# One of three maxout products folded into the output: differences of weights, W1 Wout added to y, and a new hand order

## The chip, the cores and the metric

The kernel runs on one core of one Trainium2 chip. The metric is the device time of one execution in microseconds; the median of three runs is given with the lowest and the highest. The core has five engines that run side by side and wait for each other by semaphores: TensorE (PE in the profile; PEld is its weight load), VectorE (DVE), ScalarE (ACT), GpSimd (POOL) and SyncE (SP), which here only issues DMAs. TensorE writes to PSUM, eight banks of 128 x 512 float32; the other tiles lie in SBUF.

## What is computed

Attention with a sliding window of 128 and 4 sink keys, over batch 4, 8 heads, 768 positions and head size 64, and then a feed-forward layer whose hidden value is the largest of three products (3072 tokens, model width 512, hidden width 768). Inputs and output are float32; the kernel works in bfloat16 with float32 accumulation.

```
scores = scale * np.matmul(q, k.transpose(0, 1, 3, 2))
keep = is_sink | in_window
scores = np.where(keep, scores, -1000000000.0)
scores = scores - np.max(scores, axis=-1, keepdims=True)
a = np.exp(scores)
a = a / (np.sum(a, axis=-1, keepdims=True) + 1e-09)
attn_out = np.matmul(a, v)
x = np.ascontiguousarray(attn_out.transpose(0, 2, 1, 3)).reshape(B * S, H * D)
h = np.maximum(np.maximum(x @ w1, x @ w2), x @ w3)
return (h @ w_out).astype(np.float32)
```

## The kernel before, in words

The 3072 tokens are cut into 12 chunks of 256 queries, three to a batch entry. A chunk passes through these steps, each a small function that records its instructions:

- `load(ci, what)`: three DMAs of float32 k, q and v, 512 KB each, from SP's queue. Two buffers of each. Some carry a `gate`: a tiny GpSimd write into the buffer that the DMA must wait for.
- `cast_qk`, `cast_k`, `cast_v`: to bfloat16, on whatever engine the call names. `turn` and `turn2` transpose q and k on TensorE (chunks 0 to 3), `turn_dma` by a transposing DMA (from chunk 4).
- `score`, `expo`, `mask`: key-by-query scores into two PSUM banks for each pair of heads, exponentials by ScalarE, the window mask as a product on VectorE. From chunk 6 (`NEW`) `score4`, `expo4` and `mask4` do this with smaller key blocks. `sink_score` and `sink_v` add the four sink keys.
- `av_open`, `av`, `norm`: the weighted sum of v (with a column of ones for the row sum) and the division on VectorE, which gives `x_sb`. `xpose` (TensorE) or `xpose_dma` transposes x into `xT`.
- `ffn_h(ci, fp, wi)`: one PSUM bank of x W for weight wi and the pair fp of 128-column blocks, eight matmuls of 128x256. For wi = 0 ScalarE copies it into `h_sb`; for wi = 1 and 2 VectorE takes the maximum with what is there. With `then=False` the copy or maximum is recorded later by `ffn_max`.
- `ffn_y`, or `y_open`, `y_turn` and `y_out`: h times Wout, six depth steps of 128x512 for each of two halves of the chunk. `y_turn` does it in tiles of 64 rows, in two turns. `store` writes the chunk out.

PSUM banks are handed out by `bank` and returned by `give`, in the order of recording, first in, first out: which earlier tile a new one must wait for is fixed by the order in which the steps are written. Each engine works through its own instructions in that same order. Nothing is scheduled automatically: up to chunk 4 the order is a list of calls written by hand, and from there on a loop over i (lines 897 to 956), whose iteration holds the attention of chunk n = i + 1, the h of chunk i, the y of chunk m = i - 1, the casts of chunk i + 2 (all on GpSimd except q, which ScalarE casts) and the loads of chunk i + 3. "The iteration of chunk n" below is that one.

The three weights W1, W2, W3 are loaded by GpSimd's queue in nine parts (`load_w(wi, c0, c1)`), Wout in two (`load_wo`). While they and the first chunks arrive, TensorE starts with matmuls of zeros (`warm`) and masks added ahead of the scores (`premask`).

Inside a chunk the queries lie with even and odd ones apart, since a DMA row holds two neighbouring positions. The matmul of `ffn_h` reads `xT` through a rearranged view (lines 518 to 526), so that the output rows pair up again for the store.

Of the kernel before, what the change touches and what calls it, by code (L numbers as in the profile page):

```python
# [16 lines left out]
def kernel(  # L17
# [13 lines left out]
    nc = tc.nc  # L31
# [17 lines left out]
    with tc.manual_schedule():  # L49
# [71 lines left out]
        def cast_v(ci, n, i, eng):  # L121
# [5 lines left out]
            for h in range(2):  # L127
                x, y = 64 * h + 32 * i, 64 * n + 32 * h
                eng.tensor_copy(  # L129
                    vb[ci % RING][x:x + 32, n, :, 0:D], raws[ci, "v"][y:y + 32, :, i])  # L130
# [109 lines left out]
        def masks2():  # L240
            nc.gpsimd.memset(keep, 1.0)
            for h in range(2):
                for i in range(2):
# [3 lines left out]
                        base=64 * h + i, pattern=[[-64, 2], [-1, 2], [-2, 32]],  # L247
# [3 lines left out]
                        base=-64 * h - i, pattern=[[64, 2], [1, 2], [2, 32]],  # L251
# [45 lines left out]
        def load_wo():  # L297
            x = moe_w_out.rearrange("(a p) f -> p a f", p=128)
            for a in range(0, FB, FB // 2):
                nc.gpsimd.dma_start(out=wo[:, a:a + FB // 2], in_=x[:, a:a + FB // 2])  # L300

# [68 lines left out]
        def expo4(ci, p):  # L370
            e, st = es[ci, p]
            for a in range(2):
                dst = e[:, a] if ci % CPB else e[:, a, 1:].rearrange("q s (j r) -> q (s j) r", j=2)
                nc.scalar.activation(dst, st[a], AF.Exp, scale=scale)  # L374
# [33 lines left out]
        def sink_score(ci):  # L408
# [18 lines left out]
            nc.scalar.activation(e, st, AF.Exp, scale=scale)  # L427
# [83 lines left out]
        def ffn_h(ci, fp, wi, cuts=1, eng=nc.scalar, then=True):  # L511
# [3 lines left out]
            for f in range(2):  # L515
                c0 = (2 * fp + f) * 128
                for ds in range(DS):
                    x = xTs[ci][:, ds]
                    if ci < NEW:
                        x = x.rearrange("q t (i r) -> q i t r", i=2)  # L520
                    else:
                        x = (x.rearrange("q t c -> q (t c)")
                             .rearrange("q (j i r) -> q i j r", i=2, r=32))
                    nc.tensor.matmul(  # L524
                        hp[:, f].rearrange("q (i t r) -> q i t r", i=2, r=x.shape[3]),
                        lhsT=w_sb[wi][:, ds, c0:c0 + 128], rhs=x,
# [17 lines left out]

        def ffn_y(ci, t, eng=None):
# [6 lines left out]
            for fb in range(FB):  # L552
                nc.tensor.matmul(yp, lhsT=hs[ci][:, fb, t * 128:(t + 1) * 128], rhs=wo[:, fb],  # L553
                                 start=(fb == 0), stop=(fb == FB - 1))
# [9 lines left out]
        def y_turn(ci, turn, cols):  # L564
# [6 lines left out]
            for fb in range(FB):  # L571
                for c in range(0, 128, cols):
                    for a in range(2):
                        t = a ^ turn
                        hp = slice(64 * a, 64 * a + 64)
                        x = t * 128 + c
                        nc.tensor.matmul(  # L577
                            yps[ci][t][c:c + cols], lhsT=hs[ci][hp, fb, x:x + cols],
                            rhs=wo[hp, fb], start=(turn == 0 and fb == 0),
                            stop=(turn == 1 and fb == FB - 1), skip_group_check=True)  # L580
# [13 lines left out]
        def ffn_y_part(ci, t, c0, c1, eng):  # L594
# [3 lines left out]
            for fb in range(FB):  # L598
                nc.tensor.matmul(yp, lhsT=hs[ci][:, fb, t * 128:(t + 1) * 128],  # L599
                                 rhs=wo[:, fb, c0:c1], start=(fb == 0), stop=(fb == FB - 1))  # L600
# [3 lines left out]
        def store(ci):  # L604
            nc.sync.dma_start(
                out=out[ci * 256:ci * 256 + 256].rearrange("(p i) d -> p i d", i=2), in_=ys[ci])

        def store_half(ci, i, c0=0, c1=d_model, eng=None):
            dst = out[ci * 256:ci * 256 + 256].rearrange("(p i) d -> p i d", i=2)
# [10 lines left out]

        def cast(ci):
            if ci >= NCH:
                return
            assert ci >= NEW
            if ci == NEW:
                for g in range(2):
                    cast_qk(ci, "q", g, nc.gpsimd)
            for n in range(2):
                for h in range(2):
                    for i in range(2):  # L630
                        cast_k(ci, n, h, i, nc.gpsimd)
            if ci > NEW and ci % CPB == 1:
                sink_k(ci // CPB)
            for n in range(2):
                for i in range(2):
# [364 lines left out]
```

## Time and profile before

| | us |
|---|---|
| median of 3 runs (lowest to highest) | 175.3 (175.07 to 176.21) |
| span of the profiled execution, first to last instruction | 173.5 |
| median less that span | 1.8 |

The page names no other time for the profiled execution than its span; the 1.8 us stand for what lies around it. TensorE is busy nearly all the time, and its granted clock is full in all slices. The table's first row of a group gives busy time, mean length of one instruction, then the engine's idle time ahead of such instructions and what ended it. A mean length of a matmul (0.27 us for the h matmuls) is longer than its share of TensorE's time, since matmuls overlap; the chain of work, in order of time, gives the true pace.

```profile
L524 PE MATMUL h_ps<-xT,w 128*128 128x256 bf16 x864 | 101.2, 273 | 0.1
...
L536 ACT CAST h_sb<-h_ps 128x512 bf16<-128x512 f32 x35 | 20.5, 585 | 52.2 <-PE h_ps L524 52.2
```

### The profile page before, as it was taken

Reading aid. Unit: us, or ns where it says so; the run is one execution under the profiler, and the core shown is the slowest. Engines: PE = TensorE matmul, PEld = TensorE weight load, DVE = VectorE, ACT = ScalarE, POOL = GpSimd, SP = SyncE. Lnnn points to the kernel's source line nnn. Section 1 sums busy time; section 2 is a strip of 40 time slices with the busy share of each in tenths; the row PEclk is TensorE's granted clock in tenths of the full one; section 3 lists DMA queues with packets and bytes.
Section 4 is the critical chain, followed back from the end, with each engine's and each line's share of the span. In section 5 each row is a group of like instructions: output and inputs, shape, how many; then the busy total and the mean of one; then the engine's idle time right before and its main releaser. Section 6 shows DMA issues by size and latency. Waiting matters only on the chain.

```text
span 173.5 us, 5418 instructions
## 1 busy us (share of the span) xinstructions
PE 167.7 (97%) x2225; PEld 129.2 (74%) x2225; DVE 125.1 (72%) x262; ACT 88.8 (51%) x183; POOL 110.1 (63%) x193
## 2 busy tenths in 40 slices
PE   7979999999999999999999999999999999999992
PEld 2546889857695697797797797797897896896871
DVE  3187856696697985986877977877778876776361
ACT  4598554587944615817726717627636516510210
POOL 7389507445399999999999999999998700000000
PEclk9999999999999999999999999999999999999999
DMA  4999999999996999988999969969999119017303
GB/s 134 300 289 198 216 217 252 219 274 290 292 210 118 250 264 180 252 188 220 264 186 247 264 165 254 257 163 238 257 176 274 32 34 376 21 35 272 121 2 121
DMA packets 71545, 35.22 MB, mean 203 GB/s; under 512 B 27488, under 2 KB 69984, under 8 KB 71520
## 3 DMA queue, kind: packets, MB, share of 16 engines
q1 hardware_dynamic: 65824, 31.60, 79.0%
q0 software_dynamic: 5552, 3.15, 12.8%
q8 instruction: 17, 0.28, 0.7%
q10 hardware_dynamic: 144, 0.13, 0.2%
q14 instruction: 8, 0.07, 0.1%
HBM read 25.17 MB, written 6.29 MB: 181 GB/s over the span
## 4 chain that ended last, share of the span: by engine, by line
PE 93%; DVE 3%; ACT 1%; issue 0%
PE h_ps L524 55%; PE y_ps L577 11%; PE y_ps L553 7%; PE o L471 7%; PE st L357 3%; PE warm L203 3%; PE st L331 3%; PE pt L138 2%; ACT e_sb L398 1%; PE o L453 1%; DVE x_sb L484 1%; PE sk L423 1%; PE y_ps L599 1%; DVE vb L123 1%; PE xt L496 1%; PE st L311 0%
## 5 line engine op out<-in xcount | busy, mean ns | idle before, releaser
L524 PE MATMUL h_ps<-xT,w 128*128 128x256 bf16 x864 | 101.2, 273 | 0.1
L524 PEld LDWEIGHTS <-w 128*128 128x128 bf16 x864 | 81.9, 98 | 9.9 <-issue 0.3
L540 DVE TENSOR_TENSOR h_sb<-h_sb,h_ps 128x512 bf16<-128x512 bf16 (+1 forms) x74 | 49.3, 671 | 20.0 <-PE h_ps L524 16.0
L536 ACT CAST h_sb<-h_ps 128x512 bf16<-128x512 f32 x35 | 20.5, 585 | 52.2 <-PE h_ps L524 52.2
L129 POOL CAST vb<-v_raw 32x512 bf16<-32x512 f32 x48 | 36.7, 764 | 2.8 <-DMA v_raw<-in_v_dram 0.6
L90 POOL CAST k_bf<-k_raw 32x512 bf16<-32x512 f32 x48 | 29.5, 614 | 2.2
L398 ACT ACTIVATE e_sb<-st 128x512 bf16<-128x512 f32 (+1 forms) x48 | 23.1, 588 | 0.7 <-PE st L331 0.7
L484 DVE TENSOR_TENSOR x_sb<-o,rc 128x256 bf16<-128x256 f32 x48 | 20.4, 424 | 1.6
L577 PE MATMUL y_ps<-wo,h_sb 64*64 64x512 bf16 (+1 forms) x312 | 21.1, 377 | 0.0
L471 PE MATMUL o<-vb,e_sb 128*128 128x65 bf16 x352 | 16.8, 193 | 0.4 <-ACT e_sb L398 0.4
L471 PEld LDWEIGHTS <-e_sb 128*128 128x128 bf16 x352 | 14.6, 97 | 2.8 <-issue 0.8
L123 POOL CAST vb<-v_raw 64x512 bf16<-64x512 f32 x18 | 12.4, 691 | 5.8 <-DMA v_raw<-in_v_dram 5.2
L389 DVE TENSOR_TENSOR e_sb<-e_part,msk 128x1024 bf16<-128x1024 bf16 x16 | 13.5, 865 | 3.1 <-ACT e_part L374 3.0
L406 DVE TENSOR_TENSOR e_sb<-e_sb,msk 128x1024 bf16<-128x1024 bf16 (+1 forms) x18 | 13.3, 756 | 2.1 <-ACT e_sb L398 2.0
L577 PEld LDWEIGHTS <-h_sb 64*64 64x64 bf16 (+1 forms) x312 | 9.9, 106 | 5.0
L374 ACT ACTIVATE e_part<-st 128x384 bf16<-128x384 f32 x32 | 13.1, 496 | 0.5 <-PE st L357 0.5
L553 PE MATMUL y_ps<-wo,h_sb 128*128 128x512 bf16 x54 | 13.0, 380 | 0.0
L481 DVE RECIPROCAL rc<-o 128x4 f32<-128x4 f32 x48 | 8.3, 174 | 3.5 <-PE o L471 3.4
L118 POOL CAST k_bf<-k_raw 128x512 bf16<-128x512 f32 x6 | 3.8, 647 | 9.6 <-DMA k_raw<-in_k_dram 9.4
L553 PEld LDWEIGHTS <-h_sb 128*128 128x128 bf16 x54 | 4.8, 97 | 5.6 <-DVE h_sb L540 0.9
L118 ACT CAST q_bf<-q_raw 128x512 bf16<-128x512 f32 x13 | 7.6, 621 | 2.0 <-DMA q_raw<-in_q_dram 1.9
L427 ACT ACTIVATE e_sink<-sk 128x256 bf16<-128x256 f32 x8 | 3.1, 389 | 10.0 <-PE sk L423 10.0
(90 smaller groups left out, 144.2 us busy)
## 6 DMA issues: line engine op xcount, KB each, us to landing
k_raw<-in_k_dram SPq DMA_DIRECT2D x11, 512.0 KB, 5.7
v_raw<-in_v_dram SPq DMA_DIRECT2D x11, 512.0 KB, 5.8
q_raw<-in_q_dram SPq DMA_DIRECT2D x10, 512.0 KB, 6.5
out_dram<-y_sb SPq DMA_DIRECT2D x9, 512.0 KB, 3.1
w<-in_moe_w_dram POOLq DMA_DIRECT2D x9, 256.0 KB, 6.6
q_raw<-in_q_dram SPq DMA_DIRECT2D x4, 256.0 KB, 7.7
out_dram<-y_sb SPq DMA_DIRECT2D x1, 1024.0 KB, 5.2
wo<-in_moe_w_out_dram POOLq DMA_DIRECT2D x2, 384.0 KB, 7.4
```

The source lines that it names most:

```text
L90: f(bfs[ci, "k"][x:x + 32, :, n], raws[ci, "k"][y:y + 32, :, i].rearrange("q (p a) d -> q p a d", a=2))
L123: eng.tensor_copy(vb[ci % RING][64 * i:64 * i + 64, n, :, 0:D], raws[ci, "v"][64 * n:64 * n + 64, :, i])
L129: eng.tensor_copy(vb[ci % RING][x:x + 32, n, :, 0:D], raws[ci, "v"][y:y + 32, :, i])
L389: nc.vector.tensor_mul(x.rearrange("q a (t s) c -> q (a t) s c", t=2), y, msk2)
L398: nc.scalar.activation(e[:, a, lo:], st[a][:, lo:], AF.Exp, scale=scale)
L471: nc.tensor.matmul(o[:, t, a], lhsT=e[:, a, s], rhs=vb[cv % RING][:, n, 2 * p + a], start=first, stop=True, skip_group_check=True)
L484: nc.vector.tensor_mul(xs[ci][:, p], o[:, :, :, 0:D], rc.unsqueeze(3).to_broadcast([128, 2, 2, D]))
L524: nc.tensor.matmul(hp[:, f].rearrange("q (i t r) -> q i t r", i=2, r=x.shape[3]), lhsT=w_sb[wi][:, ds, c0:c0 + 128], rhs=x, start=(ds == 0 ...
L536: (nc.scalar.copy if eng is nc.scalar else eng.tensor_copy)(dst, hp)
L540: nc.vector.tensor_max(dst[:, x], dst[:, x], hp[:, x])
L553: nc.tensor.matmul(yp, lhsT=hs[ci][:, fb, t * 128:(t + 1) * 128], rhs=wo[:, fb], start=(fb == 0), stop=(fb == FB - 1))
L577: nc.tensor.matmul(yps[ci][t][c:c + cols], lhsT=hs[ci][hp, fb, x:x + cols], rhs=wo[hp, fb], start=(turn == 0 and fb == 0), stop=(turn == 1 ...
```

## The change

max(x W1, x W2, x W3) equals x W1 + max(0, x (W2 - W1), x (W3 - W1)). So from chunk 1 on (`SHIFT = 1`) h holds only the second term, which takes two products instead of three, and y becomes h Wout + x (W1 Wout).

- `diff` forms W2 - W1 and W3 - W1 in bfloat16, three column parts each, on VectorE. `turn_w` transposes W1 on TensorE (eight 128x128 blocks at a time, copied out by ScalarE) and `join` multiplies the result by Wout, 128 rows of `wg` = W1 Wout at a time.
- In `ffn_max` the first of the two products goes through a Relu on ScalarE, in place of the copy; the second is a maximum on VectorE as before. `ffn_h(ci, fp, 0)` is gone from chunk 1 on.
- `terms` lists the matmuls of y: four depth steps of x times `wg`, then the six of h times Wout. `ffn_y`, `y_turn` and `ffn_y_part` go through that list.
- The queries keep their natural order from chunk 6 on: the exponentials (`expo4`, and `sink_score`'s) write them in place of the split order, and `ffn_h` reads `xT` plainly. Chunks 0 to 5 keep the split order, and their `store` becomes two DMAs, one for the even and one for the odd rows.
- In the loop, now written out call by call, the two casts of v's second half (`cast_v(ci, 1, 0)` and `(ci, 1, 1)`, four instructions) go from GpSimd to ScalarE, from chunk 6 on.
- The opening is recorded in another order. Two warm-up matmuls go. `cast_qk(0, 'k', 0)` goes from ScalarE to VectorE, `turn2(1, 'q', 0)`'s copy from VectorE to ScalarE. `expo(0, 1)` comes after a k cast, one part of W2 is loaded one step sooner, `load(4, 'k')` stands ahead of `load(4, 'q')`, and more v casts of chunk 2 stand ahead of the load of chunk 3.

```diff
+        def diff(wi, g, eng, ds=slice(0, DS)):
+            c = slice(256 * g, 256 * g + 256)
+            eng.tensor_sub(dw[wi][:, ds, c], w_sb[wi][:, ds, c], w_sb[0][:, ds, c])
+
+        def turn_w(g, eng):
+            pt = bank([128, 2, DS, 128], BF16, "pt")
+            for f in range(2):
+                c0 = (2 * g + f) * 128
+                for ds in range(DS):
+                    nc.tensor.transpose(pt[:, f, ds], w_sb[0][:, ds, c0:c0 + 128], ident)
+            (nc.scalar.copy if eng is nc.scalar else eng.tensor_copy)(wT[:, 2 * g:2 * g + 2], pt)
+            give(pt)
+
+        def join(ds, eng):
+            gp = bank([128, d_model], F32, "y_ps")
+            for fb in range(FB):
+                nc.tensor.matmul(gp, lhsT=wT[:, fb, ds], rhs=wo[:, fb],
+                                 start=(fb == 0), stop=(fb == FB - 1))
+            (nc.scalar.copy if eng is nc.scalar else eng.tensor_copy)(wg[:, ds], gp)
+            give(gp)
...
-                dst = e[:, a] if ci % CPB else e[:, a, 1:].rearrange("q s (j r) -> q (s j) r", j=2)
-                nc.scalar.activation(dst, st[a], AF.Exp, scale=scale)
+                dst = (e[:, a].rearrange("q j (r i) -> q j i r", i=2) if ci % CPB else
+                       e[:, a, 1:].rearrange("q s (j r i) -> q (s j) i r", j=2, i=2))
+                nc.scalar.activation(dst, st[a].rearrange("q j (i r) -> q j i r", i=2),
+                                     AF.Exp, scale=scale)
...
-                        hp[:, f].rearrange("q (i t r) -> q i t r", i=2, r=x.shape[3]),
-                        lhsT=w_sb[wi][:, ds, c0:c0 + 128], rhs=x,
+                        hp[:, f], lhsT=(dw if ci >= SHIFT else w_sb)[wi][:, ds, c0:c0 + 128],
+                        rhs=xTs[ci][:, ds].rearrange("q t r -> q (t r)"),
...
-            if wi == 0:
+            if ci >= SHIFT and wi == 1:
+                for f in range(cuts):
+                    x = slice(2 * f // cuts, 2 * (f + 1) // cuts)
+                    if eng is nc.scalar:
+                        nc.scalar.activation(dst[:, x], hp[:, x], AF.Relu)
...
+        def terms(ci, t):
+            ops = [(xTs[ci][:, ds, t], wg[:, ds]) for ds in range(DS)] if ci >= SHIFT else []
+            return ops + [(hs[ci][:, fb, t * 128:(t + 1) * 128], wo[:, fb]) for fb in range(FB)]
...
-            for fb in range(FB):
-                nc.tensor.matmul(yp, lhsT=hs[ci][:, fb, t * 128:(t + 1) * 128], rhs=wo[:, fb],
-                                 start=(fb == 0), stop=(fb == FB - 1))
+            ops = terms(ci, t)
+            for j, (x, w) in enumerate(ops):
+                nc.tensor.matmul(yp, lhsT=x, rhs=w, start=(j == 0), stop=(j == len(ops) - 1))
...
+            for t in range(2):
+                nc.sync.dma_start(out=x[128 * t:128 * t + 128].rearrange("(r i) d -> i r d", i=2),
+                                  in_=ys[ci][:, t])
...
-        warm(4)
+        warm(2)
...
+        turn_w(2, nc.scalar)
         xpose(1, 1, nc.scalar, (0, 1, 3, 2))
+        diff(1, 2, nc.vector)
+        diff(1, 1, nc.vector)
+        turn_w(1, nc.scalar)
+        diff(1, 0, nc.vector)
         ffn_max(0, 2, 1)
...
         ffn_y(0, 0)
         ffn_y(0, 1)
+        join(0, nc.scalar)
+        join(1, nc.vector)
         av_open(2)
```

Two places show what the new order does on the engines that TensorE waits for. The first is VectorE in the opening, from the copy of chunk 1's first half of `xT` on: `h_sb<-h_sb,h_ps` are maxima, `dw` is a difference of weights, `kT` a transposed key copy, `q_bf` and `k_bf` are casts of chunk 2. Before:

```order
L498 COPY xT<-xt 128x4x128
L540 TENSOR_TENSOR h_sb<-h_sb,h_ps 128x512 x4
L149 COPY kT_71<-pt 128x2x256
L540 TENSOR_TENSOR h_sb<-h_sb,h_ps 128x512 x3
L118 CAST q_bf<-q_raw 128x2x2x2x64
L540 TENSOR_TENSOR h_sb<-h_sb,h_ps 128x512 x3
L406 TENSOR_TENSOR e_sb<-e_sb,msk 128x1024
```

And now:

```order
L533 COPY xT<-xt 128x4x128
L310 TENSOR_TENSOR dw_111<-w_108,w_107 128x4x256 x3
L576 TENSOR_TENSOR h_sb<-h_sb,h_ps 128x512 x3
L118 CAST k_bf<-k_raw 128x2x2x2x64
L149 COPY kT_71<-pt 128x2x256
L310 TENSOR_TENSOR dw_112<-w_109,w_107 128x4x256
L576 TENSOR_TENSOR h_sb<-h_sb,h_ps 128x512
L310 TENSOR_TENSOR dw_112<-w_109,w_107 128x4x256
L118 CAST q_bf<-q_raw 128x2x2x2x64
```

The three parts of W2 - W1 stand ahead of the first maxima of chunk 0, a k cast came from ScalarE, and two parts of W3 - W1 stand ahead of the cast of q.

The second is ScalarE in the iteration of chunk 7: the sink's exponentials, those of the window, y's copy, then h of chunk 6 and the casts of later chunks. Before:

```order
L427 ACTIVATE e_sink<-sk 128x256
L374 ACTIVATE e_part<-st 128x384 x8
L591 COPY y_sb<-y_ps 128x512
L536 CAST h_sb<-h_ps 128x512 x3
L118 CAST q_bf<-q_raw 128x2x2x2x64 x2
```

And now:

```order
L462 ACTIVATE e_sink<-sk 128x4x2x32
L404 ACTIVATE e_part<-st 128x6x2x32 x8
L632 COPY y_sb<-y_ps 128x512
L568 ACTIVATE h_sb<-h_ps 128x512 x2
L129 CAST vb_77<-v_raw 32x8x64 x4
L118 CAST q_bf<-q_raw 128x2x2x2x64 x2
L568 ACTIVATE h_sb<-h_ps 128x512
```

The three copies of h became three Relus, and four v casts and the two q casts stand between the second and the third.

More of the change, by code (lines that the diff above doesn't have):

```diff
@@ L564, in y_turn @@
         def y_turn(ci, turn, cols):
-            for fb in range(FB):
+            ops = [terms(ci, t) for t in range(2)]
+            for j in range(len(ops[0])):
                 for c in range(0, 128, cols):
@@ L619, in pool_gate @@
             nc.gpsimd.memset(dst, 0.0)
[L621 to L635, printed above, removed]
-                    cast_v(ci, n, i, nc.gpsimd)
         load(0, 'q', part=1, parts=2)
```

705 lines of the change are left out of this document (558 added, 147 removed).

## The prediction, made before the changed kernel was run

> **What bounds the kernel now.** I read the engine table first, then the share of engines in the chain of work that ended last, then that chain in order of time. The columns of the chain are start, length and piece, in us.
>
> ```profile
> PE 167.7 (97%) x2225; PEld 129.2 (74%) x2225; DVE 125.1 (72%) x262; ACT 88.8 (51%) x183; POOL 110.1 (63%) x193
> ...
> PE 93%; DVE 3%; ACT 1%; issue 0%
> ```
>
> ```profile
> 15.88 1.03 PE h_ps L524 x8
> ...
> 33.23 0.77 PE st L331 x18
> ...
> 36.40 2.70 PE y_ps L553 x12
> ...
> 42.14 0.45 PE pt L138 x8
> ...
> 44.33 0.44 PE st L331 x8
> ...
> 67.49 0.22 PE sk L423 x4
> ...
> 82.71 1.29 PE y_ps L577 x24
> 84.01 0.29 PE o L471 x6
> 84.30 1.75 PE h_ps L524 x16
> 86.05 0.18 PE o L471 x6
> ...
> 87.97 0.37 PE o L471 x12
> ...
> 92.71 0.18 PE sv L437 x8
> ...
> 93.46 1.39 PE y_ps L577 x22
> ...
> 157.09 2.59 PE y_ps L553 x12
> 159.67 7.86 PE h_ps L524 x72
> ```
>
> TensorE (PE) is the bound from the first FFN matmul at 15.88 us to the end of the last y: the pieces follow each other without a gap. So the sum is made on PE, and everything else counts only where it makes PE wait. Prices per matmul come from the long pieces. An h matmul (128x256) is 7.86 / 72 = 0.109 us. A y matmul (128x512) is 2.59 / 12 = 0.216 us; the y turns of four 64x64 tiles cost the same per column (24 quarters, six whole matmuls, take 1.29). A 128x128 transpose is 0.45 / 8 = 0.056 us.
>
> **The sum on PE.** From chunk 1 on each chunk multiplies by two weights instead of three: 3 column pairs x 2 blocks x 4 depth steps = 24 h matmuls fewer. Eleven chunks: 264 x 0.109 = 28.8 us removed. The added term x(W1 Wout) puts 4 depth steps ahead of the 6 of h in each of two y tiles: 8 matmuls of 512 columns per chunk, 88 x 0.216 = 19.0 us added. The product W1 Wout itself is new: 24 transposes of W1 (1.3 us) and 4 x 6 matmuls of 512 columns (5.2 us). Net: 28.8 - 19.0 - 1.3 - 5.2 = 3.3 us saved on PE. A chunk saves 24 x 0.109 - 8 x 0.216 = 0.9 us, and chunk 1 to 11 pay off 6.5 us of preparation: most of the gain of seven chunks is spent before it starts.
>
> **What of it doesn't arrive: the opening.** The preparation stands between 22 and 46 us. Ahead of the scores of chunk 2 (piece at 33.23), PE loses three groups of eight h matmuls (2.6 us) and gains the transposes (1.3 us), so it would come there 1.3 us sooner, at 31.9. But these scores need the last part of q of chunk 2, which is in flight. The first row is from the DMA issues around 19.4 us, the second from SyncE's timeline, the third and fourth from VectorE (DVE) and ScalarE (ACT).
>
> ```profile
> q_raw<-in_q_dram SPq DMA_DIRECT2D x1, 256.0 KB, 11.7
> 19.20 1.37 SPq L107 DMA_DIRECT2D q_raw<-in_q_dram  x1
> 31.01 0.43 DVE L118 CAST q_bf<-q_raw 128x512 bf16<-128x512 f32 x1
> 32.40 0.58 ACT L142 COPY qT<-pt 128x512 bf16<-128x512 bf16 x1 [0.51 <-PE pt L138]
> ```
>
> It lands at 19.20 + 11.7 = 30.9. The cast (0.43), the four transposes (0.2, and about as long to drain) and the copy (0.58) end near 32.5; one h group runs beside the copy. So the scores start near 32.6 and PE idles about 0.65 us. The DMA engines are full in that stretch (below), and SyncE's rows of loads stand in the same order up to chunk 3, so I don't expect q earlier. The bounds are 0 (q lands 0.7 sooner) and 1.3 (nothing gained there). For the same reason I give nothing for the reordered start: two warm-up matmuls fewer, a k cast on VectorE instead of ScalarE and one W2 load ahead of the sink keys may bring 15.88 forward by some tenths, but PE would only wait longer for q.
>
> Six differences W2-W1, W3-W1 go to VectorE, 128x1024 each; no such subtraction is in the trace, and the nearest rows are the mask products of that size, 0.757 and 0.865 us.
>
> ```profile
> L406 DVE TENSOR_TENSOR e_sb<-e_sb,msk 128x1024 bf16<-128x1024 bf16 x14 | 10.3, 757 | 2.1 <-ACT e_sb L398 2.0
> L389 DVE TENSOR_TENSOR e_sb<-e_part,msk 128x1024 bf16<-128x1024 bf16 x16 | 13.5, 865 | 3.1 <-ACT e_part L374 3.0
> L540 DVE TENSOR_TENSOR h_sb<-h_sb,h_ps 128x512 bf16<-128x512 bf16 x70 | 47.8, 685 | 19.8 <-PE h_ps L524 16.0 <-ACT h_sb L536 1.9 <-PE o L471 0.3
> ...
> L118 ACT CAST q_bf<-q_raw 128x512 bf16<-128x512 f32 x13 | 7.6, 621 | 2.0 <-DMA q_raw<-in_q_dram 1.9
> ...
> L129 POOL CAST vb<-v_raw 32x512 bf16<-32x512 f32 x48 | 36.7, 764 | 2.8 <-DMA v_raw<-in_v_dram 0.6
> ```
>
> What the other engines have free there, and in two iterations of the loop, stands in the view by windows: after the stretch and its length come busy us of PE, PEld, DVE, ACT and POOL, then the clock, the DMA share and GB/s.
>
> ```profile
> 16.00:33.20 17.20, 17.20 (x200) 14.96 (x200) 11.51 (x24) 9.14 (x18) 7.48 (x16) 1.00 1.32 226
> 33.20:44.30 11.10, 11.10 (x135) 6.94 (x136) 8.36 (x19) 9.01 (x18) 6.35 (x14) 1.00 1.12 272
> ...
> 80.50:92.70 12.20, 12.20 (x185) 9.83 (x189) 9.42 (x19) 6.59 (x14) 11.30 (x19) 1.00 1.07 236
> 92.70:105.90 13.20, 13.20 (x226) 10.76 (x225) 10.69 (x20) 6.87 (x15) 12.37 (x19) 1.00 0.96 226
> ```
>
> Six differences cost 4.5 to 5.2 us of VectorE, and three maxima of chunk 1 less (0.685 each) give 2.1 back before 33.2: 11.5 of 17.2 becomes about 14 of 16.6. I cost them at nothing; the cover is the maxima of chunk 0 standing behind them, whose banks PE needs only two or three groups later. It is gone if the third difference waits for W2's first columns: then three maxima queue behind it, and PE runs out of banks, up to one h group (0.9 us), of which the wait for q hides most. The three copies of transposed W1 (128x1024, at most two of the 0.58 copies each) meet a ScalarE that is busy 9.1 of 17.2 us, and the joins' four copies to SBUF come in a stretch in which ScalarE and VectorE have 2 to 3 of 11 us free, and which the joins lengthen: nothing. The joins need the whole of Wout, as y(0) does now.
>
> **What doesn't arrive: the loop.** From chunk 5's iteration (67.49) on, POOL gives half of its v casts to ScalarE: four casts of 32x512, put between the second Relu and the third. The third Relu frees a bank, and the last maximum, which needs that Relu, another.
>
> ```profile
> 86.08 0.58 ACT L536 CAST h_sb<-h_ps 128x512 bf16<-128x512 f32 x1 [0.29 <-PE h_ps L524]
> ...
> 90.61 1.14 ACT L118 CAST q_bf<-q_raw 128x512 bf16<-128x512 f32 x2
> ...
> 91.94 1.49 DVE L540 TENSOR_TENSOR h_sb<-h_sb,h_ps 128x512 bf16<-128x512 bf16 x2 [0.26 <-PE h_ps L524]
> ```
>
> ScalarE starts such casts every 0.52 us (two in 1.14). Laid over the iteration that begins at 80.5: the second Relu starts at 86.08, then six casts, so the third starts at 86.08 + 0.5 + 6 x 0.52 = 89.7 and ends at 90.3; PE's h group for it is done at 84.01 + 0.29 + 1.75 + 0.18 + 0.87 + 0.37 + 2 x 0.87 = 89.2. The last maximum runs to 91.0 (0.69). PE finishes its last h group at 90.1, and sink and scores (0.75) bring it to 90.8, where the y of the next iteration takes the two banks that the third Relu and the last maximum free: a wait of 0.2. This pairing of banks comes where sink_v stands ahead, in the iterations of chunk 7 and 10, and so now: at 93.46 y takes 1.39 where others take 1.29. Elsewhere y gets banks freed earlier, and the loop hides it. I take 0.35 us in all; the bounds are 0 and 0.5 in each of six iterations, 3.0. ScalarE would be busy about 6.9 + 2.1 = 9 us of 12: enough room.
>
> The remaining edits at nothing: the exponentials write pairs of queries interleaved. No ScalarE row writes with such a step; the nearest with small pieces is the q cast, 0.62 against 0.58, so from nothing to 0.04 on eight exponentials, 0.3 us of the 3 us that ScalarE has free per iteration. y's x-part stands first, which gives the last maximum 0.86 us more before it is needed. Stores of chunks 0 to 5 become two DMAs on SyncE; they stand behind the transposes of x, and only those of chunks 0 and 1 ahead of one, the last, whose result PE needs after the two y of chunk 10. POOL loses four casts of 0.764 and goes from 12.4 to about 9.3 us per iteration; nobody waits for it on PE's chain now, nor then.
>
> Sum: 3.3 - 0.65 - 0.35 = 2.3 us off; I take 0.1 for small waits between 50 and 58 us, where fewer h groups stand between scores and their masks. The profiled span of 173.5 us becomes 171.3. The median of the runs is 175.3, 1.8 above the span; with the same 1.8 the forecast is 173.1.
>
> **The rivals.**
> (1) The opening hides nothing: q lands as early as PE comes, or the earlier start counts. Then the whole 3.3 us and a few tenths arrive: 171.7. For it: only one transfer stands in the way. Against: the DMA share of 1.32 in that stretch.
> (2) ScalarE becomes the late engine in the loop: its casts wait for v or its Relus come late, 0.3 us in six iterations, 1.8 us: 174.9. It decides once the third Relu is more than 0.4 us later than worked out. For it: three quarters of an iteration busy, and v casts ahead of a Relu. Against: only 6.9 of 13.2 us busy now, and most banks come from elsewhere.
> (3) The other side: the DMA engines set the loop's pace. The loop now takes (157.09 - 67.49) / 7 = 12.8 us per chunk, and should take 11.9. Its DMA share averages 1.01 over the two window rows above, against 1.12 while the loads run with hardly a pause (33.2 to 44.3): an estimate of 12.8 x 1.01 / 1.12 = 11.5 us per chunk for the DMA engines alone. If it is 12.8 after all, the seven iterations save nothing, 6.3 us go, and the time is 173.1 + 6.3 = 179.4; half of that, 176.2, is likelier. It decides where DMA needs more than 11.9 us per chunk. Against: x, k and q are transposed an iteration ahead, and the opening, longer by some 6 us, lets the loads run ahead.
> (4) PE's clock comes up late.
>
> ```profile
> 1.26 3.60 PE warm L203 x8
> ...
> 5.29 1.46 PE warm L203 x4
> 6.75 0.32 PE st L311 x2
> 7.07 0.45 PE pt L138 x8
> ...
> 8.20 2.40 ACT e_sb L398 x6
> ```
>
> The first eight warm-up matmuls take 0.45 each and the transposes at 7.07 0.056, so the pace doubles somewhere near 6.2 us, though the granted clock reads 1.00 in every window row. With two warm-up matmuls fewer PE has a gap of up to some 0.3 us near 6.3. Should the doubling come later for it, the 1.45 us of PE pieces from 6.75 to 8.20, where ScalarE's exponentials take over, would take twice as long: 1.45 us, of which the wait for q hides 0.65: 173.9. The Trainium skill, "TensorE: Matmul & The Clock Gate", Part 1 (The HAM clock gate), speaks against the edit: the full clock is released only after a free-running window of about 3.4 us has been busy. By that rule a whole window could be lost if the gap counts as idle. The warm-up rows agree with a release after a window; whether a short gap matters no row shows.
> (5) The change does little because something else holds PE: 175. PE's chain without gaps speaks against it.
>
> **How the numbers follow.** The forecast with its bounds (172.4 to 174.0) has 0.57, rival 1 0.13, rival 2 0.14, rival 3 0.09, rival 4 0.04, rival 5 0.03. About 1% (1.75 us) is what a measurement of this kernel can tell from no change, so faster means below 173.55: four fifths of the forecast and rival 1, 0.59. Within 1% are the rest of the forecast and rivals 2, 4 and 5, 0.32. Slower is rival 3, 0.09. The range reaches from rival 1 to the near edge of rival 3: 171.6 to 175.2.
>
> **What would show it.** Right: h matmuls 600 instead of 864 at 0.109 us; iterations of 11.9 us; PE idle for half a microsecond just before the scores of chunk 2, waiting for the q cast; the scores of chunk 3 some 6 us later than now (44.33) and the loop's first iteration 2 to 3 us later. Wrong: iterations still near 12.8 with PE waiting for kT or xT (rival 3) or for ScalarE's Relu or copies (rival 2); no idle time at 31 us (rival 1); the transposes at 7 us at 0.1 each (rival 4). The forecast fails if the differences hold up PE's banks between 24 and 28 us.

## The result, and the profile after

| | kernel before | kernel after |
|---|---|---|
| median of the runs, us | 175.61 (175.07 to 176.21, 4 runs) | 212.49 (212.23 to 213.15, 4 runs) |
| span of the profiled execution, us | 173.5 | 210.9 |
| mean granted TensorE clock in it | 1.00 | 0.924 |

The changed kernel is slower: the ratio is 1.210, with a 95% interval of 1.207 to 1.214. Executions more than 1.5% above the fastest of their kernel count as slow; the medians here and below include them, the ratios and intervals leave them out. The prediction was 173.1 us, with a range of 171.6 to 175.2.

The first three lines are from the page of the kernel after: the engine table, TensorE's clock in the 40 slices (tenths), and the share of engines in the chain that ended last.

```profile
PE 173.5 (82%) x2245; PEld 123.1 (58%) x2251; DVE 106.4 (50%) x236; ACT 112.0 (53%) x213; POOL 92.8 (44%) x169
...
PEclk9999999999999999999589959985999999995698
...
PE 64%; DMA 19%; SPq 7%; POOL 2%; DVE 2%; issue 1%; ACT 1%; POOLq 0%; ACTq 0%
```

Before, TensorE was busy in 97% of the span and made up 93% of the chain. Now it is busy in 82%, transfers and the queue that issues them hold a quarter of the chain, and the clock drops in the second half. What TensorE waited for (us in total, times, longest):

```profile
PE st L386 <- DMA kT<-k_bf: 13.6, 3, 5.7
PE h_ps L553 <- DMA xT<-x_sb: 10.0, 1, 10.0
PE sk L454 <- DMA qT<-q_bf: 4.9, 2, 3.3
```

All three are transposes by DMA, issued from SyncE's queue. The chain in order of time (start, length, piece) shows where, and what each wait leaves behind:

```profile
71.26 0.22 PE sk L454 x4
...
96.84 5.63 DMA kT<-k_bf
...
104.14 3.60 PE y_ps L618 x31
...
108.33 2.21 PE y_ps L618 x39
...
123.65 4.18 PE y_ps L618 x39
...
178.96 1.48 PE h_ps L553 x14
180.43 15.45 DMA xT<-x_sb
...
195.93 6.96 PE h_ps L553 x48
```

The loop starts at 71.26, 3.8 us later than before. Its last h group ends near 181.6 (178.96 and 24 matmuls of 0.109), so seven iterations take 110.3 us where they took 89.6: 20.7 us more. What follows takes 210.9 - 181.6 = 29.3 us where it took 16.4: 12.9 more, of which 10.0 are the wait for xT. The three add up to the 37.4 us between the spans. A wait costs more than its own length: behind it 39 quarters of y take 4.18 us in place of 2.21, because the clock has dropped.

What stands ahead of those transposes is seen on SyncE. Before (start, us, line, what, count), then after, the same stretch of the same iteration:

```profile
77.68 1.24 SPq L503 DMA_TRANSPOSE xT<-x_sb  x1
79.02 0.52 SPq L605 DMA_DIRECT2D out_dram<-y_sb  x1
79.64 1.57 SPq L188 DMA_TRANSPOSE qT<-q_bf  x1
...
82.13 0.63 SPq L107 DMA_DIRECT2D q_raw<-in_q_dram  x1
82.87 3.90 SPq L188 DMA_TRANSPOSE kT<-k_bf  x1
```

```profile
82.31 1.23 SPq L538 DMA_TRANSPOSE xT<-x_sb  x1
83.59 1.32 SPq L652 DMA_DIRECT2D out_dram<-y_sb  x2
85.01 8.49 SPq L188 DMA_TRANSPOSE qT<-q_bf  x1
...
96.84 2.68 SPq L188 DMA_TRANSPOSE kT<-k_bf  x1
...
170.33 9.11 SPq L652 DMA_DIRECT2D out_dram<-y_sb  x4
180.43 11.28 SPq L538 DMA_TRANSPOSE xT<-x_sb  x1
```

Behind the two stores the issue of one transpose takes 8.49 us in place of 1.57, and so kT's issue comes 14.5 us after that of xT, not 5.2. At the end five stores stand ahead of the last xT, four of them of the new shape. Last, three stretches in the view by windows (the last three columns are the clock, the share of the 16 DMA engines, and GB/s):

```profile
97.00:102.40 5.40, 0.29 (x4) 0.13 (x4) 0.00 (x0) 0.66 (x2) 2.32 (x4) 0.79 1.19 289
102.40:108.30 5.90, 5.59 (x93) 3.50 (x97) 2.87 (x4) 3.29 (x8) 5.54 (x9) 0.61 0.54 138
```

```profile
182.00:183.00 1.00, 1.00 (x6) 0.47 (x5) 0.44 (x2) 0.00 (x0) 0.00 (x0) 1.00 0.13 49
```

TensorE works for 0.29 us of the first stretch, in two waits of 3.35 us (for qT) and 4.00 us (for kT). The clock falls inside that stretch and is 0.50 from 100.2 to 107.0; 0.61 is the mean of the second stretch, which ends at full clock. Where only the stores run, the share is 0.13 and the rate 49 GB/s. A share of 0.13 is two engines of 16. At 49 GB/s a store of 256 KB takes 5.3 us, so a pair takes near 11.

### The profile page after: what moved, and what is told of

The parts are those of the page before. It is cut to its first block, busy times and chain, and to the rows that moved or that the text cites. A ratio compares the mean times of both kernels' runs of the same rounds, so it can differ in the third digit from the quotient of the medians.

```text
span 210.9 us, 5444 instructions
## 1 busy us (share of the span) xinstructions
PE 173.5 (82%) x2245; PEld 123.1 (58%) x2251; DVE 106.4 (50%) x236; ACT 112.0 (53%) x213; POOL 92.8 (44%) x169
## 4 chain that ended last, share of the span: by engine, by line
PE 64%; DMA 19%; SPq 7%; POOL 2%; DVE 2%; issue 1%; ACT 1%; POOLq 0%; ACTq 0%
PE h_ps L553 24%; PE y_ps L618 17%; DMA kT<-k_bf 9%; DMA xT<-x_sb 7%; PE y_ps L594 6%; SPq L107 5%; PE o L506 4%; PE st L386 3%; DMA v_raw<-in_v_dram 3%; PE y_ps L326 2%; PE st L360 2%; SPq L188 2%; PE y_ps L641 1%; PE pt L138 1%; POOL w L292 1%
## 5 line engine op out<-in xcount | busy, mean ns | idle before, releaser
L553 PE MATMUL h_ps<-xT,dw 128*128 128x256 bf16 x528 | 64.7, 277 | 10.1 <-DMA xT<-x_sb 10.0
L553 PEld LDWEIGHTS <-dw 128*128 128x128 bf16 x528 | 50.4, 99 | 17.3 <-DMA xT<-x_sb 10.5
L576 DVE TENSOR_TENSOR h_sb<-h_sb,h_ps 128x512 bf16<-128x512 bf16 (+1 forms) x41 | 26.5, 658 | 46.2 <-PE h_ps L553 20.1
L568 ACT ACTIVATE h_sb<-h_ps 128x512 bf16<-128x512 f32 x33 | 19.6, 598 | 37.0 <-PE h_ps L553 37.0
L386 PE MATMUL st<-qT,kT 64*64 64x128 bf16 (+3 forms) x256 | 8.5, 254 | 13.6 <-DMA kT<-k_bf 13.6
L118 ACT CAST q_bf<-q_raw 128x512 bf16<-128x512 f32 x13 | 7.5, 616 | 21.7 <-DMA q_raw<-in_q_dram 21.7
L618 PE MATMUL y_ps<-wg,xT 64*64 64x512 bf16 (+1 forms) x208 | 18.5, 434 | 0.6 <-DVE h_sb L576 0.4
L618 PEld LDWEIGHTS <-h_sb 64*64 64x64 bf16 (+1 forms) x312 | 13.6, 120 | 8.3 <-issue 2.4
L129 POOL CAST vb<-v_raw 32x512 bf16<-32x512 f32 x24 | 17.3, 723 | 1.4 <-DMA v_raw<-in_v_dram 0.2
L386 PEld LDWEIGHTS <-kT 64*64 64x64 bf16 x256 | 7.1, 122 | 16.0 <-DMA kT<-k_bf 14.2
L129 ACT CAST vb<-v_raw 32x512 bf16<-32x512 f32 x24 | 14.8, 617 | 0.4
L594 PE MATMUL y_ps<-wo,h_sb 128*128 128x512 bf16 x53 | 12.9, 379 | 0.1
```

The lines of the kernel that those rows point to most:

```text
L129: (eng.copy if eng is nc.scalar else eng.tensor_copy)(vb[ci % RING][x:x + 32, n, :, 0:D], raws[ci, "v"][y:y + 32, :, i])
L386: nc.tensor.matmul(st[a][64 * h:64 * h + 64, at:at + q1 - q0] .rearrange("q j (i r) -> q j i r", i=2), lhsT=x[hp, p, n, h], rhs=qT[ci % RI ...
L553: nc.tensor.matmul(hp[:, f], lhsT=(dw if ci >= SHIFT else w_sb)[wi][:, ds, c0:c0 + 128], rhs=xTs[ci][:, ds].rearrange("q t r -> q (t r)"), ...
L568: nc.scalar.activation(dst[:, x], hp[:, x], AF.Relu)
L576: nc.vector.tensor_max(dst[:, x], dst[:, x], hp[:, x])
L594: nc.tensor.matmul(yp, lhsT=x, rhs=w, start=(j == 0), stop=(j == len(ops) - 1))
```

## The experiments

Kernels of one group ran on the same chip beside the kernel before, whose medians there were 175.49, 175.87, 175.63 and 175.56 us. Each ratio is to that kernel, with its 95% interval.

| run | us | ratio |
|---|---|---|
| e1: after, stores of chunks 0 to 5 cut by 64 rows | 179.72 | 1.021 (1.012 to 1.030) |
| e2: before, with the stores of after | 208.6 | 1.187 (1.180 to 1.193) |
| e3: before, two stores, 128 outermost | 175.99 | 1.002 (0.999 to 1.005) |
| e4: after, only stores of chunks 3 to 5 recut | 190.81 | 1.087 (1.079 to 1.094) |
| e14: before, stores with 4 outermost | 189.07 | 1.074 (1.069 to 1.079) |
| e5: e1, load of q one iteration earlier | 178.56 | 1.013 (1.007 to 1.019) |
| e6: e1, v casts back on GpSimd | 178.66 | 1.015 (1.007 to 1.023) |
| e9: e1, stores of 3 to 8 behind the loads | 175.4 | 0.997 (0.993 to 1.001) |
| e10: e5 and e9 | 175.6 | 0.996 (0.992 to 1.001) |
| e11: e10, a third of W3 loaded later | 175.25 | 0.999 (0.996 to 1.003) |
| e12: e10, two v casts on VectorE | 175.59 | 0.999 (0.996 to 1.002) |
| e13: e11 and e12 | 176.24 | 1.002 (0.998 to 1.005) |
| e15: e10, two v casts ahead of the first Relu | 174.24 | 0.991 (0.987 to 0.994) |
| e16: e15 and e11 | 174.29 | 0.991 (0.987 to 0.994) |

### What makes it 37 us slower: e1 to e4, and e14

The theory: the stores of chunks 0 to 5 are slow since their slowest index, `i`, counts two. The rivals: that there are twice as many stores, with shorter rows, and that the rest of the change is what delays the transposes. e1 takes the changed kernel and lets the rows count slowest; the same bytes go to the same places in as many DMAs:

```diff
-            for t in range(2):
-                nc.sync.dma_start(out=x[128 * t:128 * t + 128].rearrange("(r i) d -> i r d", i=2),
-                                  in_=ys[ci][:, t])
+            for i in range(2):
+                nc.sync.dma_start(out=x.rearrange("(t r i) d -> i r t d", t=2, i=2)[i],
+                                  in_=ys[ci][64 * i:64 * i + 64])
```

> The changed kernel with only the stores of chunks 0 to 5 cut another way: two DMAs each as before, but one for the even and one for the odd queries, so that the view's outermost dimension is 64 partitions instead of 2. Theory A (a store whose outermost dimension is 2 runs on 2 of 16 DMA engines at about 51 GB/s, and the transposes behind it on SyncE's queue wait): the stretches at 51 GB/s go, PE no longer waits for kT and xT, and the time is that of the forecast, 172 to 175 us. Rival B (two stores of 2 KB rows in place of one of 4 KB rows, or their number on SyncE's queue, hold the transposes): still above 200. Rival C (the ScalarE casts and the new order hold the loop anyway): between 180 and 200.

It took 179.72 us: 32.8 of the 36.9 us between the medians are gone. The 172 to 175 us expected were not reached; the other 4 us over the kernel before are the next group's question.

e2 goes the other way. It gives the kernel before, with nothing else of the change, the stores of the kernel after (in its own query order, so that rows of chunks 0 to 5 land permuted).

```diff
-            nc.sync.dma_start(
-                out=out[ci * 256:ci * 256 + 256].rearrange("(p i) d -> p i d", i=2), in_=ys[ci])
+            x = out[ci * 256:ci * 256 + 256]
+            if ci >= NEW:
+                nc.sync.dma_start(out=x.rearrange("(p i) d -> p i d", i=2), in_=ys[ci])
+                return
+            for t in range(2):
+                nc.sync.dma_start(out=x[128 * t:128 * t + 128].rearrange("(r i) d -> i r d", i=2),
+                                  in_=ys[ci][:, t])
```

> The kernel before, with only the stores of chunks 0 to 5 replaced by the changed kernel's two DMAs each (outermost dimension 2, 256 KB; the one store of chunks 0 and 1 becomes four). The rows of these chunks land in another order, so this part of the output differs. Theory A: each takes about 5 us at 51 GB/s and holds the transposes behind it, so the time rises by 30 to 40 us to 205 to 215. Rival C: within 2 us of 175.6.

It took 208.6 us, 33.1 more than the kernel before, and TensorE waited 13.8 us for kT and 9.1 for xT. The stores alone bring it about.

e3 keeps e2's number of stores and writes the same count of rows, of 2 KB each, with the 128 partitions outermost:

```diff
             for t in range(2):
-                nc.sync.dma_start(out=x[128 * t:128 * t + 128].rearrange("(r i) d -> i r d", i=2),
-                                  in_=ys[ci][:, t])
+                nc.sync.dma_start(out=x.rearrange("(p i) d -> i p d", i=2)[t], in_=ys[ci][:, t])
```

> The kernel before, with the stores of chunks 0 to 5 as two DMAs each with 2 KB rows, but with 128 partitions outermost. Theory A: nothing is slow about the number of stores or the row length; 175 to 176.5 us. Rival B: 205 to 215, like the store with outermost dimension 2.

175.99 us, a ratio of 1.002 whose interval holds 1: neither the number of stores nor their rows cost anything. That rival falls. The transpose of q behind such a pair takes 1.29 us to issue. The rows of e3's stores lie two rows apart in the output, as those of e2's do, so it isn't that step either.

e4 tells the stores in the loop (chunks 3 to 5) from those at the end (0 to 2):

```diff
+            if ci >= 3:
+                for i in range(2):
+                    nc.sync.dma_start(out=x.rearrange("(t r i) d -> i r t d", t=2, i=2)[i],
+                                      in_=ys[ci][64 * i:64 * i + 64])
+                return
             for t in range(2):
```

> The changed kernel with the stores of chunks 3, 4 and 5 cut into 64 rows outermost and those of chunks 0, 1 and 2, at the end, left as they are. Theory A: the loop runs as forecast (iterations of about 12 us), and only the last transpose of x waits: four stores of 5 us stand ahead of it, so 15 to 20 us more than the kernel with all stores recut: 188 to 194. Rival B or C: above 200.

190.81 us: the six stores at the end cost 11.1 us over e1 (15 to 20 had been expected), those in the loop the other 21.7 up to 212.49.

e14, run later, asks the same again, the count of the slowest index or the step between rows: e2 with a slowest index of 4, whose rows lie four apart.

```diff
-                nc.sync.dma_start(out=x[128 * t:128 * t + 128].rearrange("(r i) d -> i r d", i=2),
+                nc.sync.dma_start(out=x[128 * t:128 * t + 128].rearrange("(r i) d -> i r d", i=4),
```

> The kernel before, with the stores of chunks 0 to 5 as two DMAs each whose slowest index counts 4 in place of 2 (rows of the output land permuted). If the slowest index sets how many of the 16 DMA engines work, 4 engines move 256 KB in about 2.5 us where 2 took 5; a stretch in which nothing else moves shows a share of 0.25 and some 100 GB/s in place of 0.13 and 49 to 53. Of the waits for kT, 5.8 us at the longest with 10 us of stores ahead, 5 us of stores leave up to 1 us: 175.5 to 179. If the step between the rows in memory is what is slow, it stays near 208.

A window near its end, where only stores run:

```profile
164.00:165.00 1.00, 1.00 (x18) 0.92 (x15) 0.53 (x2) 0.59 (x1) 0.00 (x0) 1.00 0.26 102
```

Twice the index gives twice the share and twice the rate, as expected, though the step is larger: in these stores the slowest index sets the number of engines. The expected time (175.5 to 179) was too low. It took 189.07 us, since TensorE still waits 9.0 us for kT in three iterations: pairs of stores of 5 us keep SyncE from issuing qT for 5.88 us.

### What holds e1 at 179.7: e5, e6, e9 and e10

e1's chain, in the iteration of chunk 6's scores, up to y in the next one:

```profile
88.67 6.80 DMA q_raw<-in_q_dram
...
95.57 1.14 ACT q_bf L118 x2
96.71 0.50 ACT h_sb L568
...
97.23 0.70 DVE h_sb L576
...
97.97 3.81 PE y_ps L618 x37
```

The load of q, the cast on ScalarE that waits for it, the third Relu behind that cast, the last maximum, y: one after the other, and y then runs at a slower clock. On SyncE that load is issued 6.2 us after the transposes of x:

```profile
82.47 1.23 SPq L538 DMA_TRANSPOSE xT<-x_sb  x1
83.80 1.35 SPq L652 DMA_DIRECT2D out_dram<-y_sb  x2
85.25 2.74 SPq L188 DMA_TRANSPOSE qT<-q_bf  x1
...
88.67 0.58 SPq L107 DMA_DIRECT2D q_raw<-in_q_dram  x1
```

Before it was 4.45 us (77.68 to 82.13). The second store takes 0.8 us more to issue, and the qT behind it 1.2. Three theories: the place of the load of q in the queue; ScalarE's v casts (rival 2); the bytes on the DMA engines (rival 3). e5 moves only the loads of q:

```diff
         load(8, 'k')
-        load(8, 'q')
         turn_dma(7, 'k')
         load(8, 'v')
+        load(9, 'q')
```

> The changed kernel with the stores of chunks 0 to 5 in 64 rows (179.7 us), and in the loop the load of q of each chunk recorded one iteration earlier, behind the load of v. Late q: in the run with 64 rows the load of q is issued at 88.67, lands 6.80 us later, and casts, Relu, maximum and y follow it; y starts at 97.97, and its first 37 quarters take 3.81 us where 2.22 stand elsewhere; the same at 138.47. If that load's place in SyncE's queue is the cause, both waits go, y keeps 2.2, iterations are 12.0 to 12.3 apart from kT's waits of up to 1.5 us each, and the time is 173.5 to 175.5. DMA engines as the bound (shares of 1.06 to 1.20 in these iterations): an earlier load only makes kT or xT late; iterations stay at 13.5 and the time at 178 to 181.

178.56 us: a miss, at most 1.2 us off where 4 to 6 were expected (the intervals of e1 and e5 overlap). The chain shows the reason. q is no longer in it, and in its place stand kT in three iterations (TensorE waits for it in four, 3.7 us in all) and the k casts of GpSimd ahead of it. The load of k comes no sooner: it is issued 7.8 us behind the transposes of x (82.07 to 89.86), where e1 had 5.6 (82.47 to 88.03). The earlier load of q now stands just ahead of those transposes, whose issue takes 3.28 us in place of 1.23:

```profile
75.92 7.85 DMA kT<-k_bf
...
128.41 7.01 DMA kT<-k_bf
```

e6 puts the four v casts of each iteration back on GpSimd:

```diff
-        cast_v(7, 1, 0, nc.scalar)
+        cast_v(7, 1, 0, nc.gpsimd)
...
-        cast_v(7, 1, 1, nc.scalar)
+        cast_v(7, 1, 1, nc.gpsimd)
```

> The changed kernel with the stores of chunks 0 to 5 in 64 rows, and the four v casts of each loop iteration back on GpSimd. ScalarE late (rival 2 of the prediction): the casts ahead of the third Relu are what delays it; without them the Relu comes up to 2 us sooner and the time is 174 to 176. Late q: ScalarE then waits for q instead (its q cast already waited 1.60 us for the load), and the time stays at 178.5 to 181.

178.66 us, within e1's spread (178.49 to 182.81), and TensorE's waits for kT stay at 3.0 us. The 174 to 176 of rival 2 are not reached: ScalarE's casts are not what holds e1 back.

e9 leaves the loads where they are and takes the stores out of their way:

```diff
         ffn_max(5, 2, 2)
-        store(4)
...
         load(9, 'v')
+        store(4)
```

> The changed kernel with the stores of chunks 0 to 5 in 64 rows, and the stores of chunks 3 to 8 recorded behind the next iteration's load of v, so that between the transposes of x and the loads of k and q only the transposes of q are left on SyncE. Late q: the load of q is issued some 1.5 us sooner after the transposes of x, which takes away about half of each wait: 175 to 177. DMA engines as the bound: the same bytes at another place, 178 to 181.

175.4 us, 4.3 less than e1 with the same bytes (3.1 less than e1's fastest execution), and TensorE's waits for kT fall from 3.1 us to 0.4. So what was late is everything behind the stores on SyncE, q, k and kT alike. The DMA engines' capacity is not the bound: that theory had 178 to 181.

e10 does both.

> Both of the last edits of SyncE's queue: q loaded one iteration earlier and the stores of chunks 3 to 8 behind the loads. Late q: nothing is left of the waits at 97 and 138, kT comes sooner too, iterations of 12.0, loop of 84 us in place of 90.6: 172.5 to 174.0, below the kernel before. DMA engines as the bound: 178 to 181.

175.6 us, no better than e9 and above the 172.5 to 174.0 expected. No DMA is left among TensorE's waits, but the loop takes 157.03 - 72.03 = 85.0 us, not the 83.3 of the prediction's sum, and it starts at 72.03.

```profile
72.03 0.22 PE sk L454 x4
...
96.27 0.69 DVE h_sb L576
...
97.00 2.22 PE y_ps L618 x37
...
133.51 2.22 PE y_ps L618 x37
...
157.03 4.32 PE y_ps L594 x20
```

### The last 2.5 us: e11, e12, e13, e15 and e16

Two places are left: these two starts of y, to which the chain comes by way of the last maximum, 0.73 us after the scores end (96.27 to 97.00), and the opening. e11 is for the opening: it moves 256 KB of W3 out of the way of q of chunk 2.

```diff
-        load_w(2, 512, 768)
...
         cast_qk(2, 'k', 1, nc.gpsimd)
+        load_w(2, 512, 768)
         load_wo()
```

> The run with both edits of SyncE's queue (175.6 us), and the last third of W3 loaded by GpSimd behind its k cast of chunk 2, at 27.9 in place of 19.3. q late in the opening: q of chunk 2 lands up to 1.1 us sooner (256 KB fewer ahead of it, at 226 GB/s), and the scores of chunk 2 start at 33.0 to 33.4 in place of 34.06; the time is 0.5 to 1.0 us less, 174.6 to 175.1. TensorE and ScalarE late by themselves: the scores stay at 33.5 to 34.1 and the time at 175.3 to 176.0, or more if Wout, then loaded later, holds up y of chunk 0.

In its profile VectorE no longer waits for q. The scores of chunk 2 start at 32.71, where e10 had 34.06 and the prediction 32.6, and the loop starts at 71.06. But that says little: with e10's opening unchanged, the scores start at 32.75 in e6, 32.79 in e4 and 33.31 in the kernel after. The price is a later Wout. The median is 175.25 us, just above the 174.6 to 175.1 expected and 0.35 below e10, within what these runs can tell apart; e13, with the same edit, shows the price at its worst:

```profile
31.11 7.85 DMA wo<-in_moe_w_out_dram
...
39.00 2.10 PE y_ps L594 x9
```

Nine of the twelve matmuls of y of chunk 0 run from 39.0 on there, where e10 starts y at 37.3: TensorE waited 1.2 us for Wout.

e12 takes two of the four v casts of each iteration from ScalarE to VectorE:

```diff
-        cast_v(8, 1, 1, nc.scalar)
+        cast_v(8, 1, 1, nc.vector)
```

> The run with both edits of SyncE's queue, and two of the four v casts of each iteration on VectorE in place of ScalarE. In that run y of two iterations starts 0.7 us late, at 97.00 and 133.51, behind the third Relu and the last maximum. If the casts ahead of that Relu are the cause (rival 2 of the prediction at its smallest), the Relu comes 1.2 us sooner, both waits go, and the time is 174.0 to 174.6. If not: 175.3 to 176.0.

175.59 us, no change. VectorE now delays the same maximum:

```profile
94.52 0.42 DVE vb L129
...
95.73 0.70 DVE h_sb L576
...
96.47 2.22 PE y_ps L618 x37
```

e13 has the edits of e11 and e12 together.

> The two edits of the last two kernels together: 173.2 to 174.2 if both hold, 174.0 to 175.2 if one does, 175.3 to 176.0 if neither does.

176.24 us, above even the 175.3 to 176.0 of neither: no gain arrived. The profile shows both reasons just given, the maximum behind VectorE's casts and, in the opening, the wait for Wout.

e15 keeps the casts on ScalarE and moves two of them to where it idled, ahead of the iteration's first Relu:

```diff
         y_out(5, 1, nc.scalar)
+        cast_v(8, 1, 1, nc.scalar)
...
         cast_v(8, 1, 0, nc.scalar)
...
-        cast_v(8, 1, 1, nc.scalar)
```

> The run with both edits of SyncE's queue (175.6 us, span 174.1), and two of the four v casts of each iteration recorded on ScalarE ahead of the first Relu, where it idled 0.57 and 0.28 us, in place of ahead of the third. If ScalarE's order is what delays y at 97.00 and 133.51, the third Relu comes up to 0.85 us sooner, both waits (0.7 us each) go, and the time is 174.0 to 174.7. If the first and second Relu, now 0.4 to 0.7 later, hold a bank that TensorE needs, the time stays at 175.3 to 176.5.

174.24 us. The maximum is no longer in the chain: y starts as the scores end, though its first 38 quarters still take 2.32 us where 40 take 2.16 elsewhere. The loop, from 71.17, ends at 155.04: 83.9 us, 1.1 less than e10.

```profile
95.75 2.32 PE y_ps L618 x38
...
131.43 2.32 PE y_ps L618 x38
...
155.04 4.32 PE y_ps L594 x20
```

e16 is e15 with e11's edit.

> The same with the last third of W3 loaded behind the k cast of chunk 2 (that edit alone gave 175.25). If ScalarE's order is the cause of the two waits: 173.6 to 174.6; if not: 175.0 to 176.5.

174.29 us: the opening's edit adds nothing that these runs can tell. e15 is the version that beats both kernels, the kernel before by 0.9% (interval 0.6% to 1.3%). The new algorithm is kept as it was changed; what differs from the changed kernel is the cut of the stores and the place of stores, loads of q and v casts in their queues.

## Why the prediction was wrong

**The step that failed: "Stores of chunks 0 to 5 become two DMAs on SyncE; they stand behind the transposes of x".** It was costed at nothing, by their place in the queue. Their shape was not looked at. The slowest index of the new pattern counts 2, and two of 16 engines carry the store (0.13, 49 GB/s). The Trainium skill says so in "DMA: Bandwidth & Descriptors", section "Why a DMA increments its semaphore by 16 and not by 1": the engines used are the largest number up to 16 that divides the slowest dimension, not of size 1, of both sides. The runs with 2 and with 4 agree. Nor does being behind xT protect it: qT, the loads of k and q, and kT of the same iteration stand behind the store on the same queue. The runs put 33 of the 37 us on this one step.

**SyncE's queue behind xT.** Rival 3 had "x, k and q are transposed an iteration ahead" as evidence against late transfers. For q it doesn't hold: its load is issued and its cast runs in the same iteration, with 2 us to spare before (issued at 82.13, 6.5 us to land by the page, cast at 90.61). And with fewer h groups left, only three instead of five stand between the transposes of x and the next iteration, so the queue starts nearer to those who wait for it. That the queue starts nearer is read from the traces and was not tried by itself; what the place of the stores in it is worth e9 shows, 4.3 us. The band of rival 3, 176.2 to 179.4, ends just below e1, but for another reason than the rival gave; the DMA engines carry the same bytes in e9.

**ScalarE in the loop: 0.35 us.** The mechanism and the place were right (the third Relu behind the casts, in the iterations of chunks 7 and 10), the size was not: e10 shows 0.73 us in each, 1.5 in all, of which e15's other order got 1.1 back. The v casts had been taken at 0.52 us from start to start, and they take 0.62. Before, and then in e10:

```profile
80.83 3.26 ACT L374 ACTIVATE e_sb<-st 128x384 bf16<-128x384 f32 x8 [1.29 <-PE st L357]
```

```profile
86.97 1.96 ACT L404 ACTIVATE e_sb<-st 128x384 bf16<-128x384 f32 x4 [0.39 <-PE st L386]
...
92.08 2.50 ACT L129 CAST vb<-v_raw 32x512 bf16<-32x512 f32 x4
```

The exponentials are a bound that failed. With the interleaved write one of them lasts 0.605 us on the page of the kernel after, 0.496 on the page of the kernel before, 0.11 more where at most 0.04 had been allowed. Since they overlap, their time on ScalarE is read from start to start: eight in 3.26 us before are 0.39 apart, four in 1.96 us are 0.45, so eight cost some 0.5 us more per iteration. The write's step was not tried by itself, so it stays the likely reason, not a shown one.

**The opening: 0.65 us.** The sum, with this loss, has the loop starting at 67.49 + 1.3 + 5.2 + 3.5 - 7.9 + 0.65 = 70.2 (transposes, joins, y of two chunks, h of three). With this opening it started between 70.74 (e4) and 72.03 (e10), 1.1 to 2.4 us behind the 69.6 of no loss, where the bounds were 0 and 1.3. Much of the spread is q of chunk 2: VectorE's cast of its last part starts at 30.68 in e4, 30.94 in e6, 31.71 in e1 and 32.30 in e10, where the kernel before had 31.01. TensorE itself was late as well, by a ScalarE that casts q behind a copy; in e1:

```profile
30.73 0.40 PE L138 MATMUL pt<-ident,q_bf 128*128 128x128 bf16 x4 [0.32 <-ACT q_bf L118]
```

This is only 0.15 us sooner than the kernel before (30.88), where 1.3 us had been expected. So q was rightly named: where it came as expected, the scores start at 32.75 (e6) and 32.79 (e4), close to the 32.6 given, and elsewhere up to 1.5 us later (34.06 in e10). From there to the loop it takes 38.0 us in e4, e1 and e10 alike, 0.4 more than the sum has (70.2 - 32.6). But q was not alone. In e11 and e16 VectorE no longer waits for q, and the scores, at 32.71 and 32.90, start no sooner than in e6, with TensorE still waiting 0.3 us for ScalarE's cast.

**The sum on TensorE: 3.3 us.** The prices hold: 48 h matmuls in 5.24 us, ten y matmuls in 2.16, two joins in 2.59. In e15, where one wait of 0.3 us for kT is left in the loop, an iteration takes 83.9 / 7 = 11.98 us, where 11.9 was given. Its span, 172.2 us, is 1.3 us shorter than that of the kernel before. The parts agree: 3.3, less 1.6 in the opening (71.17 in place of 69.6 without any loss), less 0.6 in the loop (83.9 in place of 83.3), is 1.1.

**The rest.** The differences of weights delayed no bank: no wait of TensorE in these profiles names them. Rivals 1 and 5 fall with the result. Of rival 4 nothing showed in the opening, but the clock came in elsewhere. In the kernel after it was 0.50 from 100.2 to 107.0, in and behind a wait for kT, and y took twice as long; the Trainium skill, "TensorE: Matmul & The Clock Gate", Part 1, has the clock halve after an idle window of some 3.4 us. The trace agrees in so far as the clock falls within each of the waits for kT and xT, the longest 5.7 and 10.0 us. But in these runs the window need not be wholly idle. In e14, with no wait above 3.2 us, the clock falls three times, and TensorE had worked 0.7 to 1.2 us of the 3.4 us ahead of each fall. In e1 it had worked 1.5 of 3.4 us, and the clock was 0.50 from 98.4 to 101.8 after waits of 1.24, 0.34 and 0.35 us; 2.35 of 3.4 us in the iteration at 136 cost nothing.

## What to carry to other kernels

Read the shape of every DMA that a change touches, not only its bytes and its place: with 2 or 4 as the slowest index two or four engines carry it, with 64 or 128 the 33 us were gone. Then list what stands behind it on the same queue, down to the wait that TensorE meets, and the time between; a faster loop shortens that time by itself. When a repaired change still gives nothing, look for the second-latest queue: here e12 only moved the wait to another engine, and e15, which used an engine's idle time, took the maximum out of the chain.

## What the runs showed of the hardware

- A store with a slowest index of 2 ran on two engines at 49 GB/s, one with 4 on four at 102: 24.5 to 25.5 GB/s for each engine.
- A transfer of few engines holds up the issue of those behind it on its queue, of other kinds too: the transposes of q took 1.29 us to issue behind two stores with 128 outermost (e3), 5.0 to 5.9 behind two on four engines (e14), 7.4 to 8.5 behind two on two (the kernel after).
- In the kernel after, TensorE's clock fell to 0.50 during a wait for kT and stayed there for 6.8 us (100.2 to 107.0, 120.6 to 127.5 and 141.1 to 147.9). 39 quarters of y behind such a wait took 4.18 us in place of 2.21, so the slow stretch added some 2 us there.
- Waits need not be long for it: three of 1.24, 0.34 and 0.35 us within 3.4 us brought the clock to 0.50 for 3.4 us (e1), and 37 quarters of y took 3.81 us in place of 2.22.
